# Turning queries and keys of three batches by transposing transfers instead of on TensorE

## The chip, the cores and the metric

The kernel runs on one core of a Trainium2 chip. The metric is the device time of one execution in microseconds (us), from the first to the last instruction as the device counts it. The kernel before was timed three times: 1011.01, 1011.4 and 1011.7 us. One further execution was taken by the hardware profiler; it ran 1008.57 us, and its records span 1006.8 us.

The engines are called as in the profile: PE is TensorE's matmul, PEld its weight load, DVE VectorE, ACT ScalarE, POOL GpSimd, SP SyncE, whose queue issues nearly all DMAs. A letter q after an engine's name is its queue. L252 is line 252 of the kernel before.

## What is computed

Two parts follow each other: attention in which a query sees only the keys that were assigned to the same of 16 centroids, and a feed-forward block with a squared Relu. All tensors are float32.

```python
batch, n_heads, seq, head_dim = (4, 8, 768, 64)
...
q_assign = np.argmax(np.einsum('bhsd,hcd->bhsc', q_n, c_n), axis=-1)
k_assign = np.argmax(np.einsum('bhsd,hcd->bhsc', k_n, c_n), axis=-1)
mask = q_assign[:, :, :, None] == k_assign[:, :, None, :]
scores = scale * np.matmul(q, k.transpose(0, 1, 3, 2))
scores = np.where(mask, scores, -1000000000.0)
...
attn = attn / (np.sum(attn, axis=-1, keepdims=True) + 1e-09)
return np.matmul(attn, v).astype(np.float32)
...
x = np.ascontiguousarray(attn_out.transpose(0, 2, 1, 3)).reshape(B * S, H * D)
h = x @ w_in
r = np.maximum(h, 0.0)
return ((r * r) @ w_out).astype(np.float32)
```

Scores need both queries and keys with the head's 64 columns on the partitions, so each 128x128 piece of q and k has to be turned once. That turning is what the change is about.

## The kernel before

**Pairs and units.** Two heads of one batch make a pair, whose 2 x 64 columns fill the 128 partitions of a turned piece. There are 16 pairs: 0 to 3 belong to batch 0 (HP = 4), 4 to 15 to batches 1 to 3. A pair has 12 pieces of 128 positions, six of q and six of k. The work of a pair is cut into six units (pair, h, c): h is the half of the queries, c = 0, 2, 4 the pair of key pieces. For batch 0 all first halves come before all second halves; from pair 4 on a pair's six units follow each other, which takes some 34 us. Each unit traces its scores (L370), and two units later its product with v (`times_v`, L433).

**A unit.** `scores` makes eight matmuls into two PSUM tiles `sc`, ACT takes the exponential (L397, two instructions of 768 columns), and for batches 1 to 3 DVE masks by comparing cluster numbers (L401, four instructions), from PSUM into `ex`. POOL adds up the masked values (L411, L413). `last_exp` keeps the latest exponential, so that work can be tied behind it on ACT: `tc.issue_after(last_exp[0])` fixes the order of issue on the engine and adds no wait.

**Preparing a pair.** `load_qk` (L100) loads q and k of a pair into two tiles of the pool `loads`, which has four buffers under one tag. `turn` (L245) turns them in three parts: four transposes on PE (L252) into a PSUM tile `pt` and one copy by ACT (L254) into `qkT`; after part 2 it loads the pair after the next. `qkT` has two buffers for these pairs. `logits` (L262) multiplies the turned pieces with the centroids, `route` (L275) finds the number of the nearest one on DVE, and `spread` (L333) writes the numbers as a row to DRAM (L342) and loads them back onto all partitions as `qid` (L343). Batch 0 uses `turn_onehot` instead of `spread`.

**The order of the preparation.** `prep` (L348) returns these steps as a list, and the main loop (L712) takes up to three entries a unit from it, where None takes an entry's place and does nothing. `next_pair` (L688) starts the preparation of pair p + 1 at the first unit of pair p, and that of pair 4 at the second half of pair 3. For pairs after 4 the list is stretched by None entries (L717 to L720): turning in the first unit, logits in the second, route in the third, spread in the fourth.

**Finishing a half.** `add_up` (L460) makes the sums `sm` on PE, their reciprocal `r` on DVE (L482), and carries it through DRAM: SP issues `far_r` (L485), `seen` (L486), waits until far_r has landed, and issues two broadcast loads `rb` (L489). `finish` (L498), a unit later, multiplies by it on DVE (L501) and so fills `xT`, the input of the feed-forward.

**The fill.** The feed-forward of batch 0 (`ffn`, L510) is not run by itself: its matmuls (`ph`, L515, and `po`, L528) are dealt out among the units as filling for PE. `ph` is read by ACT (L522, L523). Its PSUM tiles come from the pool `ps_f`, two banks that `pt`, `lg`, `lt`, `pb`, `sm`, `ph` and `po` share. The feed-forward of batches 1 to 3 (`ffn_pair`, L541, with the matmuls L607 and L638) follows after all attention.

**Who sets the order.** The code gives each engine's instructions in a rough order of priority; a planner orders them by priority and by when it reckons each to be ready, and that order is then fixed. Each engine, SP's queue too, works through its list in order: one that waits holds back all behind it.

Of the kernel before, what the change touches and what calls it, by code (L numbers as in the profile page):

```python
# [8 lines left out]
F32 = mybir.dt.float32  # L9
BF16 = mybir.dt.bfloat16  # L10
I32 = mybir.dt.int32
U32 = mybir.dt.uint32
ALU = mybir.AluOpType
ACT = mybir.ActivationFunctionType
# [3 lines left out]
P = 128  # L18
# [6 lines left out]
def kernel(  # L25
# [10 lines left out]
    nc = tc.nc  # L36

    B, H, S, D = q.shape
    C = centroids.shape[1]
    NCH = S // P  # L40
# [4 lines left out]
    HP = H // 2  # L45
    NB = NCH // 2
    TB = NB * P
    NG = B * HP
# [10 lines left out]
    loads = ctx.enter_context(tc.tile_pool(name="loads", bufs=4))  # L59
    loads_v = ctx.enter_context(tc.tile_pool(name="loads_v", bufs=2))  # L60
    qktp = ctx.enter_context(tc.tile_pool(name="qktp", bufs=2))
# [13 lines left out]
    dram = ctx.enter_context(tc.tile_pool(name="dram", bufs=2, space=bass.MemoryType.DRAM))  # L75
# [21 lines left out]
    raw = {}  # L97
    raw_v = {}

    def load_qk(pair):  # L100
        if pair >= NG:
            return
        b, hp = divmod(pair, HP)
        raw[pair] = []
        for name, src in (("q_raw", q), ("k_raw", k)):
            t = loads.tile([P, NCH, 2 * D], F32, name=name, tag="qk")
            for e in range(2):
                (nc.scalar if pair == 0 and src is k else nc.sync).dma_start(
                    t[:, :, D * e : D * (e + 1)],
                    src[b, 2 * hp + e].rearrange("(p j) d -> p j d", p=P),  # L110
                )
            raw[pair].append(t)
# [15 lines left out]
    for fr in range(DFF // NW):  # L128
        for a in range(KT):
            cols = slice(fr * NW, (fr + 1) * NW)  # L130
# [110 lines left out]
    qkT = {}  # L241
# [3 lines left out]
    def turn(pair, part):  # L245
        if part == 0:
            pool = qkt_early if 2 <= pair < HP else qktp
            qkT[pair] = pool.tile([P, 2 * NCH, P], F32, name="qkT")
        pt = bank("pt", [P, 4, P])
        for i in range(4):  # L250
            which, c = divmod(4 * part + i, NCH)
            nc.tensor.transpose(out=pt[:, i], in_=raw[pair][which][:, c], identity=ident)  # L252
        dst = qkT[pair][:, 4 * part : 4 * part + 4]
        nc.scalar.copy(out=dst, in_=pt)  # L254
        if part == 2:
            raw.pop(pair)
            load_qk(pair + 2)

    lgs = {}
    last_logits = {}  # L260
# [1 line left out]
    def logits(pair):  # L262
        hp = pair % HP
        lg = (bank if pair else first_bank)("lg", [P, TB])
        last_logits[pair] = together(
            dict(
                out=lg[32 * g : 32 * g + 32], lhsT=cnT[:, 2 * C * hp : 2 * C * (hp + 1)],
                rhs=qkT[pair][:, NB * g : NB * (g + 1)], start=True, stop=True,
            )
            for g in range(4)  # L270
        )
        lgs[pair] = once.tile([P, TB], F32, name="lgs")
        nc.scalar.copy(out=lgs[pair], in_=lg)

    def route(pair):  # L275
        with tc.high_priority(offset=2000):
            number(pair)
# [35 lines left out]
    def turn_onehot(pair, which):  # L313
        if pair == 0:
            pt = first_bank("po", [P, NCH, P], BF16)
        else:
            pt = ps_f.tile([P, NCH, P], BF16, name="po", tag="f")
        for c in range(NCH):
            nc.tensor.transpose(
                out=pt[:, c],  # L320
                in_=oh[:, c % NB, 2 * which + c // NB].rearrange("p e c -> p (e c)"),
                identity=ident_b,
            )
        dst = qid[pair][1][:, which]
        src = pt.rearrange("p c n -> p (c n)")
        if which == 0 and pair == 0:
            nc.vector.tensor_copy(out=dst, in_=src)
        elif which == 0:
            nc.scalar.copy(out=dst, in_=src)
        else:  # L330
            nc.scalar.activation(out=dst, in_=src, func=ACT.Copy, bias=-BIG, scale=BIG)

    def spread(pair):  # L333

        src, dst = qid[pair]
        n = 4 * NB
        pb = ps_f.tile([n, P], BF16, name="pb", tag="f")
        nc.tensor.transpose(out=pb, in_=src.rearrange("p g e i -> p (g e i)"), identity=ident_b)
        row = once.tile([n, P], BF16, name="row", tag="b")
        nc.scalar.copy(out=row, in_=pb)  # L340
        far = dram.tile([n, P], BF16, name="far")
        nc.sync.dma_start(far, row)  # L342
        nc.sync.dma_start(  # L343
            dst.rearrange("p g e n -> p (g e n)"),
            far.rearrange("r n -> (r n)").partition_broadcast(P),
        )

    def prep(pair):  # L348
        return [
            lambda: turn(pair, 0), lambda: turn(pair, 1), lambda: turn(pair, 2),  # L350
            lambda: logits(pair), lambda: route(pair),
        ] + (
            [lambda i=i: turn_onehot(pair, i) for i in range(2)] if pair < HP
            else [lambda: spread(pair)]
        )

# [1 line left out]
    last_exp = [None]  # L360
# [327 lines left out]
    def next_pair(u):  # L688

        pair, h, c = units[u]  # L690
        if c == 0 and pair + 1 < NG and h == 0 and (pair + 1) not in qkT:
            if pair + 1 < HP or pair >= HP:
                return pair + 1
        if c == 0 and h == 1 and pair == HP - 1:
            return pair + 1
        return None

    to_round = iter(range(len(weights)))
# [7 lines left out]
    ahead = []  # L706
# [5 lines left out]
    for u in range(len(units) + LAG + 2):  # L712
        if u < len(units):
            pair, h, c = units[u]
            if (p := next_pair(u)) is not None:
                ahead.extend(prep(p))
                if p > HP:  # L717

                    t0, t1, t2, lg, rt, *sp = ahead
                    ahead = [t0, t1, t2, lg, None, None, rt, None, None, *sp]  # L720
            if c == 0 and u + 3 < len(units) and units[u + 3][0] not in raw_v:
                load_v(units[u + 3][0])

            with behind_first(u):
                scores(pair, h, c)
        done = None
        if LAG <= u < len(units) + LAG:
            pair, h, c = units[u - LAG]
            times_v(pair, h, c)
            if c == NCH - 2:  # L730
                done = pair, h

        rounding += 4
        while rounding >= 3:
            rounding -= 3
            i = next(to_round, None)
            if i is not None:
                with tc.issue_after(last_exp[0]):
                    round_weights(i)
                if (i := next(loaded, None)) is not None:  # L740
                    load_weights(i)
            elif not later:
                early.close()
                for name, bufs in (("xT", 5), ("out", 2)):
                    later[name] = keep.enter_context(
                        tc.tile_pool(name=name + "_late", bufs=bufs, side="right",
                                     reuse_waits="tile")
                    )
        share = max(0, left[0] - RESERVE) * density(u) // max(1, sum(map(density, range(u, ENDS))))
        goal = left[0] - share  # L750
        fill_steps(share // 2)
        for _ in range(3):
            if ahead:
                with behind_first(u):
                    (ahead.pop(0) or int)()
        fill_steps(left[0] - goal)

        if not (done and first_half(*done)):
            ended.append(done)
            done = ended.pop(0)  # L760
        if done:
            pair, h = done
            with tc.high_priority(offset=1000) if pair < HP else ExitStack():
                add_up(pair, h)
            if h == 1:
                for d in (qkT, ids, qid):
                    d.pop(pair)
            if h == 1 or pair < HP:
                raw_v.pop(pair)

        now = [done] if done and wide(*done) else []
        added.append(None if now else done)
        for pair, h in now + [d for d in [added.pop(0)] if d]:
            b, hp = divmod(pair, HP)
            with tc.high_priority(offset=1000) if wide(pair, h) else ExitStack():
                finish(pair, h)
            if hp == HP - 1 and (h == 1 or b == 0):
                for half in [(b, h)] if b == 0 else [(b, 0), (b, 1)]:
                    if half in PLAIN:
                        fill.append(ffn(*half))  # L780
# [3 lines left out]
    def check_sums():  # L784
# [20 lines left out]
    wtp, tp, sp, gp = (  # L805
        fast.enter_context(tc.tile_pool(name=name, bufs=1, reuse_waits="tile"))
        for name in ("wtp", "tp", "sp", "gp")
    )
# [207 lines left out]
```

## Time and profile before

| stretch, us from the start | what runs | PE busy | ACT busy | DVE busy | POOL busy | DMA share |
|---|---|---|---|---|---|---|
| 0 to 75 | batch 0, rounding of weights | 67.05 of 75 | 53.45 | 48.15 | 21.61 | 0.83 |
| 75 to 150 | batch 0, rounding of weights | 74.50 of 75 | 46.51 | 59.13 | 53.40 | 0.46 |
| 500 to 560 | last pairs of batches 1 to 3 | 59.68 of 60 | 21.07 | 40.25 | 38.57 | 0.10 |
| 600 to 700 | feed-forward of batches 1 to 3 | 100.00 of 100 | 7.21 | 47.62 | 9.40 | 0.03 |

The stretches between, in which most of the change lies, stand in the prediction. The granted clock of PE is 1.00 throughout. The first matmul of the last stage (L607) starts at 566.53 us.

In lists of instruction groups a row gives line, engine, operation, output and input tile, shapes and count; after the first bar the busy time in us and the mean duration of one in ns; after the second the engine's idle time just before them and what ended it. A row of a timeline gives start and length in us, engine, line and operation, and in brackets the idle time before it with its releaser. A row of waits reads: who waited, for whom, us in total, times, longest.

### The profile page before, as it was taken

Reading aid. Unit: us, or ns where it says so; the run is one execution under the profiler, and the core shown is the slowest. Engines: PE = TensorE matmul, PEld = TensorE weight load, DVE = VectorE, ACT = ScalarE, POOL = GpSimd, SP = SyncE. Lnnn points to the kernel's source line nnn. Section 1 sums busy time; section 2 is a strip of 40 time slices with the busy share of each in tenths; the row PEclk is TensorE's granted clock in tenths of the full one; section 3 lists DMA queues with packets and bytes.
Section 4 is the critical chain, followed back from the end, with each engine's and each line's share of the span. In section 5 each row is a group of like instructions: output and inputs, shape, how many; then the busy total and the mean of one; then the engine's idle time right before and its main releaser. Section 6 shows DMA issues by size and latency. Waiting matters only on the chain.

```text
span 1006.8 us, 12188 instructions
## 1 busy us (share of the span) xinstructions
PE 988.9 (98%) x4583; PEld 555.7 (55%) x4583; DVE 568.6 (56%) x907; ACT 301.0 (30%) x497; POOL 378.0 (38%) x277
## 2 busy tenths in 40 slices
PE   7999999999999999999999999999999999999997
PEld 3444444334443444443333455788655888556886
DVE  4779766655555647564675775623455532566321
ACT  5876565333333453443342111000111000111000
POOL 1338764555555555465566633001232002231000
PEclk9999999999999999999999999999999999999999
DMA  9774442122212220221110000000000000000000
GB/s 246 200 215 151 144 118 72 38 77 64 82 48 66 63 73 25 77 58 48 35 58 17 28 1 1 1 21 21 21 1 0 1 21 32 12 0 1 21 22 24
DMA packets 71512, 55.46 MB, mean 55 GB/s; under 512 B 53274, under 2 KB 62870, under 8 KB 71446
## 3 DMA queue, kind: packets, MB, share of 16 engines
q1 hardware_dynamic: 69734, 54.18, 18.7%
q8 instruction: 38, 0.62, 0.3%
q10 hardware_dynamic: 1712, 0.43, 0.2%
q14 instruction: 28, 0.23, 0.1%
HBM read 48.07 MB, written 6.42 MB: 54 GB/s over the span
## 4 chain that ended last, share of the span: by engine, by line
PE 88%; DVE 5%; DMA 2%; ACT 2%; issue 2%; SPq 0%; POOL 0%; DVEq 0%; ACTq 0%
PE bank L638 22%; PE bank L607 22%; PE po L528 8%; PE ph L515 7%; PE sc L90 7%; PE av L90 6%; PE sc L93 6%; PE av L93 5%; PE pt L252 2%; DVE ex L401 1%; DMA rb<-far_r 1%; PE sm L93 1%; DVE r L482 1%; PE sm L90 1%; ACT ex L397 1%
## 5 line engine op out<-in xcount | busy, mean ns | idle before, releaser
L413 POOL TENSOR_TENSOR acc<-acc,ex 128x768 f32<-128x768 f32 x112 | 208.2, 1859 | 142.0 <-DVE ex L401 127.1
L401 DVE SCALAR_TENSOR_TENSOR ex<-qid,ids,sc 128x384 f32<-128x384 bf16 x288 | 158.2, 607 | 69.6 <-ACT sc L397 67.3
L93 PE MATMUL sc<-qkT 64*128 64x384 f32 x576 | 150.4, 502 | 0.3
L397 ACT ACTIVATE sc<-sc 128x768 f32<-128x768 f32 x144 | 108.0, 792 | 132.9 <-PE sc L93 131.5
L93 PE MATMUL av<-ex,v_raw 128*64 128x384 f32 x576 | 144.4, 495 | 0.0
L577 DVE TENSOR_TENSOR g<-bank,g 128x384 f32<-128x384 f32 x144 | 77.8, 556 | 80.4 <-PE bank L607 79.3
L596 POOL TENSOR_TENSOR w_s<-w_in 128x256 f32<-128x256 f32 x24 | 18.7, 778 | 275.9 <-PE bank L638 162.0
L528 PE MATMUL po<-w_out,gT 128*128 128x512 f32 x192 | 100.9, 627 | 0.0
L515 PE MATMUL ph<-xT,w_in 128*128 128x384 f32 x256 | 96.9, 506 | 2.2 <-DVE r L482 2.2
L638 PE MATMUL bank<-w_out,g 128*128 128x256 f32 x432 | 95.2, 379 | 0.0
L638 PEld LDWEIGHTS bank<-w_out,g 128*128 128x128 f32 x432 | 82.1, 190 | 11.8
L90 PE MATMUL sc<-qkT 64*128 64x384 f32 x192 | 87.2, 534 | 0.2 <-DVE ex L401 0.2
L577 DVE TENSOR_TENSOR osb<-bank,osb 128x256 f32<-128x256 f32 x54 | 22.1, 423 | 107.6 <-PE bank L638 102.2
L90 PE MATMUL av<-ex,v_raw 128*64 128x384 f32 x192 | 82.5, 512 | 0.0
L93 PEld LDWEIGHTS sc<-qkT 64*128 64x128 f32 x576 | 65.0, 186 | 26.3 <-issue 1.1
L515 PEld LDWEIGHTS ph<-xT,w_in 128*128 128x128 f32 x256 | 44.0, 189 | 47.1 <-issue 16.3
L607 PE MATMUL bank<-xT,w_in 128*128 128x384 f32 x192 | 69.9, 487 | 0.0
L607 PE MATMUL bank<-x_t,w_s 128*128 128x384 f32 x192 | 69.8, 486 | 0.0
L607 PE MATMUL bank<-xT,w_s 128*128 128x384 f32 x192 | 69.8, 486 | 0.0
L411 POOL TENSOR_TENSOR acc<-ex 128x768 f32<-128x768 f32 x28 | 50.8, 1814 | 47.4 <-DVE ex L401 36.1
L638 PE MATMUL bank<-w_t,g_s 128*128 128x256 f32 x288 | 65.1, 379 | 0.0
L638 PE MATMUL bank<-w_t,g 128*128 128x256 f32 x288 | 65.1, 379 | 0.0
(121 smaller groups left out, 1214.8 us busy)
## 6 DMA issues: line engine op xcount, KB each, us to landing
w_raw<-in_moe_w_in_dram SPq DMA_DIRECT2D x16, 512.0 KB
w_raw<-in_moe_w_out_dram SPq DMA_DIRECT2D x16, 512.0 KB
v_raw<-in_v_dram SPq DMA_DIRECT2D x20, 384.0 KB
q_raw<-in_q_dram SPq DMA_DIRECT2D x32, 192.0 KB
rb<-far_r SPq DMA_DIRECT2D x62, 96.0 KB
out_dram<-osb SPq DMA_DIRECT2D x23, 256.0 KB
k_raw<-in_k_dram SPq DMA_DIRECT2D x30, 192.0 KB
qid<-far SPq DMA_DIRECT2D x12, 384.0 KB
```

Source lines behind the costliest of these rows:

```text
L90: last = nc.tensor.matmul(**next(products))
L93: last = nc.tensor.matmul(**product)
L252: nc.tensor.transpose(out=pt[:, i], in_=raw[pair][which][:, c], identity=ident)
L397: last_exp[0] = nc.scalar.activation(out=t[:, 2 * i : 2 * i + 2] if pair < HP else src, in_=src, func=ACT.Exp, scale=SCALE).ins
L401: nc.vector.scalar_tensor_tensor(out=t[:, 2 * i + e], in0=qid[pair][1][:, h, e], scalar=ids[pair][:, ch % NB, 2 + ch // NB, e : e + 1], in ...
L411: nc.gpsimd.tensor_tensor(out=acc[pair, h], in0=t[:, 0:2], in1=t[:, 2:4], op=ALU.add)
L413: nc.gpsimd.tensor_tensor(out=acc[pair, h], in0=acc[pair, h], in1=t[:, 2 * i : 2 * i + 2], op=ALU.add)
L515: nc.tensor.matmul(ph, lhsT=w_in[:, kk, f * P : (f + 1) * P], rhs=xT[b, h][:, kk], start=(kk == 0), stop=(kk == KT - 1),)
L528: nc.tensor.matmul(po, lhsT=gT[f][:, i * P : (i + 1) * P], rhs=w_out[:, f], start=(f == 0), stop=(f == FT - 1),)
L577: nc.vector.tensor_tensor(out=out, in0=bank, in1=to, op=ALU.add)
L607: nc.tensor.matmul(bank, lhsT=operands[j][0][:, kk], rhs=operands[j][1][:, kk], start=(kk == 0), stop=(kk == H2 - 1),)
L638: nc.tensor.matmul(bank, lhsT=operands[j][0][:, f], rhs=operands[j][1][:, f], start=(f == 0), stop=(f == F2 - 1),)
```

## The change

For pairs 4 to 15 the transposes on PE and their copies on ACT go. In their place each 32-bit word of q and k is split into its two 16-bit halves, the halves are written to DRAM, and one transposing DMA for a pair brings them back turned:

- `split_words(pair, which)`, once for q and once for k: two copies on ACT take the low and the high halves of each row apart into a tile `flat` (each 128 x 3 x 2 x 128 halves, so 768 a partition), from every other 16-bit element of the loaded tile. Both are tied behind the latest exponential. SP then writes `flat` to the DRAM tensor `words`, 393 KB. `flat` takes buffers of the same four as the loads. After k the loads of the next pair follow.
- `turn_words(pair)`: one transposing DMA issued by SP reads the 3072 rows of 128 halves of a pair (786 KB) and writes them to `qkT`, where the two halves of a word come to lie side by side again.
- `prep` for these pairs becomes a list by itself: in the first unit `turn_words` and the splitting of the next pair's q, in the third logits and the splitting of the next pair's k, in the fourth route, in the fifth spread. Before, logits stood in the second unit, route in the third, spread in the fourth.
- Pair 4's words are split at units 12 and 15, and its preparation starts three units earlier, at the second half of pair 2. `turn` loads the pair after the next only for pairs 0, 1 and 2; from then on each `split_words` of k loads the next pair.

```diff
-            load_qk(pair + 2)
+            if pair in (0, 1, HP - 2):
+                load_qk(pair + 2)
...
+    def split_words(pair, which):
+        if which == 0:
+            words[pair] = dram.tile([2 * NCH, P, 2, 2 * D], U16, name="words")
+        flat = loads.tile([P, NCH, 2, 2 * D], U16, name="flat", tag="qk")
+        src = raw[pair][which].bitcast(U16).rearrange("p c (d two) -> p c two d", two=2)
+        half = NCH // 2
+        with tc.issue_after(last_exp[0]):
+            for cols in (slice(0, half), slice(half, NCH)):
+                nc.scalar.copy(out=flat[:, cols], in_=src[:, cols])
+        nc.sync.dma_start(
+            words[pair][NCH * which : NCH * (which + 1)].rearrange("c p two d -> p c two d"),
+            flat,
+        )
+        if which == 1:
+            raw.pop(pair)
+            load_qk(pair + 1)
+
+    def turn_words(pair):
+        qkT[pair] = qktp.tile([P, 2 * NCH, P], F32, name="qkT")
+        nc.sync.dma_start(
+            qkT[pair].rearrange("p c n -> p (c n)").bitcast(U16),
+            words.pop(pair).rearrange("c p two d -> (c p two) d"), transpose=True,
+        )
...
     def prep(pair):
...
+        split = [lambda i=i: split_words(pair + 1, i) for i in range(2 if pair + 1 < NG else 0)]
+        first, second = split or (None, None)
         return [
-            lambda: turn(pair, 0), lambda: turn(pair, 1), lambda: turn(pair, 2),
-            lambda: logits(pair), lambda: route(pair),
-        ] + (
-            [lambda i=i: turn_onehot(pair, i) for i in range(2)] if pair < HP
-            else [lambda: spread(pair)]
-        )
+            lambda: turn_words(pair), None, first, None, None, None,
+            lambda: logits(pair), None, second, lambda: route(pair), None, None,
+            lambda: spread(pair),
+        ]
...
-        if c == 0 and h == 1 and pair == HP - 1:
-            return pair + 1
+        if c == 0 and h == 1 and pair == HP - 2:
+            return HP
...
-                if p > HP:
-
-                    t0, t1, t2, lg, rt, *sp = ahead
-                    ahead = [t0, t1, t2, lg, None, None, rt, None, None, *sp]
+            if u in (HP * NCH // 2, HP * NCH // 2 + 3):
+
+                split_words(HP, int(u > HP * NCH // 2))
```

More of the change, by code (lines that the diff above doesn't have):

```diff
@@ L11 @@
 I32 = mybir.dt.int32
+U16 = mybir.dt.uint16
 U32 = mybir.dt.uint32
@@ L256, in turn @@
             raw.pop(pair)
-            load_qk(pair + 2)
+            if pair in (0, 1, HP - 2):
+                load_qk(pair + 2)
+    words = {}
+    def split_words(pair, which):
[20 more added lines that the diff above has]
+        )
     lgs = {}
@@ L348, in prep @@
     def prep(pair):
-        return [
-            lambda: turn(pair, 0), lambda: turn(pair, 1), lambda: turn(pair, 2),
-            lambda: logits(pair), lambda: route(pair),
-        ] + (
-            [lambda i=i: turn_onehot(pair, i) for i in range(2)] if pair < HP
-            else [lambda: spread(pair)]
-        )
+        if pair < HP:
+            return [
+                lambda: turn(pair, 0), lambda: turn(pair, 1), lambda: turn(pair, 2),
+                lambda: logits(pair), lambda: route(pair),
+                lambda: turn_onehot(pair, 0), lambda: turn_onehot(pair, 1),
+            ]
+        split = [lambda i=i: split_words(pair + 1, i) for i in range(2 if pair + 1 < NG else 0)]
+        first, second = split or (None, None)
+        return [
+            lambda: turn_words(pair), None, first, None, None, None,
+            lambda: logits(pair), None, second, lambda: route(pair), None, None,
+            lambda: spread(pair),
+        ]
     ex = {}
```

## The prediction

> **What bounds the kernel now.** I read the engine totals first, then the table of stretches, to see whether TensorE is full in the stretch where the change works.
>
> ```profile
> PE 988.9 (98%) x4583; PEld 555.7 (55%) x4583; DVE 568.6 (56%) x907; ACT 301.0 (30%) x497; POOL 378.0 (38%) x277
> 150.00:250.00 100.00, 98.94 (x481) 40.05 (x481) 62.02 (x101) 39.66 (x63) 54.34 (x31) 1.00 0.23 63
> 250.00:300.00 50.00, 50.00 (x244) 20.10 (x242) 27.93 (x48) 17.79 (x27) 27.76 (x16) 1.00 0.21 59
> 300.00:400.00 100.00, 98.27 (x490) 42.41 (x486) 58.94 (x95) 44.08 (x73) 52.22 (x29) 1.00 0.23 61
> 400.00:500.00 100.00, 99.13 (x488) 40.55 (x488) 59.46 (x99) 38.06 (x60) 53.77 (x31) 1.00 0.19 55
> ```
>
> In the rows of stretches the columns after start, end and length are busy us of PE, PEld, DVE, ACT, POOL, then clock, DMA share, GB/s. From 150 to 500 us PE idles 3.7 us of 350 (1.06 + 0 + 1.73 + 0.87). DVE is at about 60%, POOL at 54%, ACT at 40%, DMA at 20%. The attention of batches 1 to 3 is bound by PE, whose gaps the feed-forward of batch 0 fills: work taken off PE there should come off the end, as long as nothing new makes PE wait.
>
> Next, what the turned tiles cost PE: the groups, then one pair in the timeline (start, length).
>
> ```profile
> L252 PE MATMUL pt<-ident,k_raw 128*128 128x128 f32 x96 | 16.6, 289 | 0.3 <-ACT qkT L254 0.3
> L252 PE MATMUL pt<-ident,q_raw 128*128 128x128 f32 x96 | 16.4, 289 | 6.1 <-DMA q_raw<-in_q_dram 6.1
> L254 ACT COPY qkT<-pt 128x512 f32<-128x512 f32 x48 | 27.8, 592 | 35.9 <-PE pt L252 35.9
> ...
> 367.22 0.60 PE L252 MATMUL pt<-ident,q_raw 128*128 128x128 f32 x4
> 369.24 0.44 PE L252 MATMUL pt<-ident,q_raw 128*128 128x128 f32 x2
> 369.52 0.82 PE L252 MATMUL pt<-ident,k_raw 128*128 128x128 f32 x6
> 370.27 0.54 PE L90 MATMUL av<-ex,v_raw 128*64 128x384 f32 x1
> ```
>
> The mean of 289 ns is latency; they are pipelined. From the start at 369.24 to the next other matmul at 370.27, 8 transposes take 1.03 us, 129 ns each. The same start-to-start reading over the timeline from 130 us on gives 15.8 us for 131 of them, 120 ns each.
>
> Last, the place most open to harm: SP's order, and what waits for it.
>
> ```profile
> 364.42 0.53 SPq L485 DMA_DIRECT2D far_r<-r  x1
> 365.00 0.55 SPq L486 DMA_DIRECT2D seen<-r  x1
> 366.04 1.12 SPq L489 DMA_DIRECT2D rb<-far_r  x2
> ...
> 369.37 0.56 DVE L501 SCALAR_TENSOR_TENSOR xT<-av,rb 128x384 f32<-128x384 f32 x1 [2.44 <-DMA rb<-far_r]
> 369.84 2.18 DVE L401 SCALAR_TENSOR_TENSOR ex<-qid,ids,sc 128x384 f32<-128x384 bf16 x4
> ...
> DVE xT L501 <- DMA rb<-far_r: 54.4, 22, 5.0
> ```
>
> The reciprocals travel SBUF, DRAM, SBUF. DVE stands idle for rb at L501, 22 times and 54.4 us between 150 and 560 us, with the masking of the next scores (L401) queued behind it. Today that hardly reaches PE.
>
> **What the Trainium skill says.** "DMA: Bandwidth & Descriptors", section "DMA Transpose (X-bar)": the plain transposing DMA takes 2-byte elements only and goes through SP's or ACT's queue. So 32-bit words must be split into halves, and the transfer stands in one of the two queues; no run of before shows one. Same page, "Latency and other measured facts": 261 GB/s for such a transfer with a non-contiguous middle dimension, 350 to 400 when contiguous. The trace has only plain loads: the 256-byte rows of q and k move at some 260 to 290 GB/s in the busy slices from 437 to 446 us. Same page, "Issuing engines are not separate DMA queues": all transfers share the 16 engines; the trace agrees in that q1 carries 54.18 of 55.46 MB, far_r, rb and qid among them. "VectorE: DVE Perf Modes", "The three transpose paths": 1309 ns by DMA for one 128x128 bf16 tile, 390 ns on TensorE; this trace has 273 ns (median, f32) on TensorE.
>
> **Part by part.**
>
> *Removed from PE:* 12 pairs (4 to 15) x 12 transposes = 144 x 120 ns = **17.3 us**, all where PE is full. Their three ACT copies a pair go too (36 x 592 ns = 21.3 us of ACT), and their three turns in the two shared PSUM banks.
>
> *Added on ACT:* four copies of 128x768 halves a pair. No row shows one. From PSUM, 768 elements take 792 ns and 384 take 491, so 0.78 ns an element. A copy in SBUF reading every other word takes 690 ns for 512 (L151); 256 more make 0.89 us. Bounds: 0.82 us (523 ns of L523 for 384 plus 384 x 0.78) and 1.02 us (1.3 ns an element, from L523 to L151). I take 0.89: 3.6 us a pair against 1.8 removed, +21 us of ACT in all, at 40% busy. What counts is place: two copies, 1.8 us, right behind the exponentials of two units of six. The next exponentials come 3.5 us later or more (368.84 + 1.50 to 376.52 is 6 us), so scores don't wait. Queued behind the copies is the Relu (L522) that frees a bank for ph. Where ph is being filled, both banks turn over each 4 matmuls; after 308 us and before 175 that is some five pairs, so ten blocks. Bounds: 0 (the Relu lands in a gap) and 10 x 1.8 = 18 us. I take 3, since the pt tiles no longer compete for these banks. Where po is filled, a bank lasts 16 matmuls and nothing waits.
>
> *Added on SP and DMA:* a pair writes 786 KB of halves to DRAM in two issues and reads them back in one transposing transfer. Two issues at 0.3 to 0.65 us hide in SP's gaps: its issues fill some 8 us of a pair's 34. The writes move at about 280 GB/s, 1.4 us each. The transfer: 786 KB at 261 GB/s is an estimate of **3.0 us**; bounds 2.0 (390 GB/s) and 31.4 us (24 tiles x 1309 ns, one after another). DMA time a pair rises by 2.8 + 3.0 of 34 us, 17%, onto 20%: no bound.
>
> *What waits for it:* logits of the pair, two units after turn_words, so 11 us and more at some 5.5 us a unit. 3 us plus two or three of latency hide there. The transfer cannot start before the last scores on the old qkT buffer, which end at 364.4 in the pair shown: the moment far_r goes out. So turn_words is ready just while SP waits for far_r to land, and it can slip in ahead of rb. How much may rb be late? With the 1.03 us of transposes gone the next scores come at 375.46 - 1.03 = 374.4; their first tile needs two maskings (1.1 us), so L401 must start by 373.3 and rb land by 372.8, against 369.37 today: **3.4 us of slack**. 3.0 us fits, narrowly; I book 1 us in all. For the other half of a pair (h = 1), rb lands at 353.53 and a 1.4 us write of words stands against about 2 us of slack.
>
> *Moved:* load_qk of the next pair goes one pair ahead instead of two, but still some four units before its copies: nothing. Spread comes one unit later (fourth instead of third of six) with two units left to land 384 KB, which go in about 2 us at 421 to 427: nothing. Preparing pair 4 three units earlier falls into the weight rounding; SP waits at L138 are up to 7.1 us there and happen once: 0 to 5 us, I take 0, as two units last 14 us.
>
> *Sum:* -17.3 + 3 + 1 = **-13.3 us**: the span of 1006.8 becomes 993.5. That profiled run took 1008.6 us, the timed ones 1011.0 to 1011.7; on their median of 1011.4 I forecast **998**.
>
> **Rivals.**
>
> *A: the transfer holds back rb (slower).* Place: turn_words between far_r and rb, on SP or in the rings. Price: the transfer's length beyond 3.4 us, 12 times. It eats the whole gain from 3.4 + 17.3/12 = 4.8 us on, 162 GB/s. At half the skill's rate, 6 us: 12 x 2.6 = 31 us against 17.3, so 1011.4 + 14 = **1025**. For it: far<-row already slips between seen and rb at 387.42, and no run of before shows what turning costs beyond a plain load of the same rows. Against: half of the halves' rb (those of h = 1) are issued two units later, and at 391.51 xT stands behind three maskings without a wait.
>
> *B: copies in ACT's way (small gain).* The Relus behind copies cost PE ten times 1.2 us: 1011.4 - 17.3 + 12 = **1006**. For it: ACT serves both banks and the scores in one queue. Against: 60% idle.
>
> *C: transposes one tile at a time.* 31.4 us a pair against some 13 us until logits: 12 x 18 = 220 us, about **1215**. For it: the 1309 ns. Against: that is one small tile, whose latency needn't add up.
>
> *D: nothing comes off.* PE's gaps return elsewhere: **1011**. For it: the waits for rb on DVE. Against: 3.7 us of idle in 350, with fill at hand.
>
> **How the numbers follow.** Forecast 0.50 (992 to 1003), B 0.14 (1003 to 1009), D 0.06, A 0.25 (1014 to 1050), C 0.05. A measurement of this kernel tells about 0.2%, 2 us, from no change. Faster 0.50 + 0.14 = 0.64; same 0.06; slower 0.25 + 0.05 = 0.30. Range 991 to 1030: above it lie C and about half of A, below it 2 in 100. The likeliest case alone: 992 to 1003.
>
> **What would show it.** Right: no L252 after 150 us, PE still 98% or more busy to 500 us, the first matmul of L607 near 553 instead of 566.5 us, ACT copies of 0.8 to 1.0 us, waits for rb on DVE not much above 54 us. A: transposing transfers over 5 us, rb issued behind them, PE waiting for L401. B: PE waits for L522. C: PE waits at lg. The forecast is wrong if PE's idle time between 150 and 560 us grows by more than 10 us.

## The result and the profile after

The changed kernel takes 994.58 us (median of 4 runs, 994.2 to 997.46), the kernel before 1011.54 us beside it. The ratio is 0.9839, with a 95% interval from 0.9821 to 0.9858: 17.0 us faster. The forecast was 998, with 992 to 1003 for its own case.

The two profiled executions differ by less: spans of 1006.8 and 992.6 us, 14.2 us; a second profile of the changed kernel, taken later, spans 991.0 us, 15.8 us less than before. In some executions PE's first matmuls take about twice as long and all that follows comes 3.0 us later (shown in the last section): these three profiles don't have that, while most timed executions of before probably do and most of after don't, which only their times suggest. So 14.2 to 15.8 us is the like-for-like gain; where a span below has those 3.0 us in it, the text says so.

The totals and the stretches of the changed kernel; the columns after start, end and length are busy us of PE, PEld, DVE, ACT, POOL, then clock, DMA share, GB/s. Line numbers are now those of the changed kernel, 38 further down in the part after `turn_words` (L553 is L515 of before, L439 is L401, L527 is L489, L539 is L501).

```profile
PE 973.4 (98%) x4439; PEld 540.7 (54%) x4439; DVE 561.7 (57%) x907; ACT 315.9 (32%) x509; POOL 377.4 (38%) x277
150.00:250.00 100.00, 97.47 (x457) 37.50 (x457) 65.44 (x103) 44.80 (x66) 56.16 (x32) 1.00 0.44 108
250.00:300.00 50.00, 49.22 (x223) 17.93 (x222) 29.35 (x50) 19.54 (x28) 27.69 (x16) 1.00 0.49 116
300.00:400.00 100.00, 99.98 (x485) 42.37 (x486) 57.30 (x99) 50.88 (x81) 55.29 (x31) 1.00 0.46 113
400.00:500.00 100.00, 99.08 (x469) 37.16 (x470) 65.07 (x107) 41.49 (x61) 57.50 (x32) 1.00 0.39 98
```

PE has 144 instructions fewer and 15.5 us less to do (988.9 to 973.4), and idles 4.3 us of the 350, against 3.7 before. So nearly all that left PE came off the end: the first matmul of the last stage (L645, before L607) starts at 551.99 instead of 566.53 us, 14.5 us earlier. ACT has 15 us more, and the DMA share doubled to 0.39 to 0.49; neither is anywhere near full.

The instructions of the change, from the lists of what touches the tiles `flat` and `qkT`; after the count come the shortest, median and longest duration in ns:

```profile
L274 ACT COPY flat<-q_raw x24: 814/836/848, 73.4 to 456.2; 128x768 uint16<-128x768 uint16 x24
L275 SPq DMA_DIRECT2D words<-flat x24: 378/400/582, 79.4 to 466.8; - x24
L285 SPq DMA_TRANSPOSE qkT<-words x12: 3099/3805/4917, 102.8 to 482.5; - x12
```

A copy takes 0.84 us. The transposing transfer occupies SP's queue for 3.8 us at the median, where plain loads take 0.3 to 0.75 at their medians (a few up to 3 us): nothing else is issued from it in that time.

Where it stands, in the timeline of the changed kernel around the switch from one pair to the next (start and length in us):

```profile
350.64 0.59 PE L94 MATMUL sc<-qkT 64*128 64x384 f32 x1
352.24 4.02 SPq L285 DMA_TRANSPOSE qkT<-words  x1
355.70 0.35 PE L91 MATMUL sm<-acc,ups 128*32 128x192 f32 x1
356.16 0.59 PE L91 MATMUL sc<-qkT 64*128 64x384 f32 x1
357.68 0.54 SPq L523 DMA_DIRECT2D far_r<-r  x1
358.27 0.53 SPq L524 DMA_DIRECT2D seen<-r  x1
358.52 1.56 ACT L274 COPY flat<-q_raw 128x768 uint16<-128x768 uint16 x2
359.31 1.12 SPq L527 DMA_DIRECT2D rb<-far_r  x2
...
362.69 0.56 DVE L539 SCALAR_TENSOR_TENSOR xT<-av,rb 128x384 f32<-128x384 f32 x1 [2.49 <-DMA rb<-far_r]
```

The last scores of the old pair (350.64) free the buffer, the transfer goes out at once and lets SP go at 356.26, and only at 357.68 does SP send far_r. The two do not meet. In all ten pairs from 6 on the transfer starts 4.8 to 6.3 us ahead of far_r; only pair 5's, at 144.89, stands between seen and rb. DVE's waits for rb between 150 and 560 us are 42.8 us in 15, fewer than before.

### The profile page after: what moved, and what is told of

It reads as the page before. It is cut to its first block, busy times and chain, and to the rows that moved or that the text cites. A ratio compares the mean times of both kernels' runs of the same rounds, so it can differ in the third digit from the quotient of the medians.

```text
span 992.6 us, 12019 instructions
## 1 busy us (share of the span) xinstructions
PE 973.4 (98%) x4439; PEld 540.7 (54%) x4439; DVE 561.7 (57%) x907; ACT 315.9 (32%) x509; POOL 377.4 (38%) x277
## 3 DMA queue, kind: packets, MB, share of 16 engines
q1 hardware_dynamic: 125798, 73.06, 28.1%
## 4 chain that ended last, share of the span: by engine, by line
PE 92%; DVE 2%; DMA 2%; ACT 2%; issue 1%; SPq 0%; DVEq 0%; ACTq 0%
PE bank L676 22%; PE bank L645 22%; PE po L566 9%; PE ph L553 8%; PE sc L91 7%; PE av L91 7%; PE sc L94 7%; PE av L94 6%; PE sm L94 1%; PE sm L91 1%; PE lg L91 1%; PE lt L314 1%; ACT ex L435 1%; DMA rb<-far_r 1%; DVE ex L439 1%
## 5 line engine op out<-in xcount | busy, mean ns | idle before, releaser
L451 POOL TENSOR_TENSOR acc<-acc,ex 128x768 f32<-128x768 f32 x112 | 205.7, 1837 | 113.1 <-DVE ex L439 100.4
L439 DVE SCALAR_TENSOR_TENSOR ex<-qid,ids,sc 128x384 f32<-128x384 bf16 x288 | 158.5, 606 | 68.3 <-ACT sc L435 59.2
L553 PE MATMUL ph<-xT,w_in 128*128 128x384 f32 x256 | 96.3, 506 | 0.5 <-DVE r L520 0.5
L645 PE MATMUL bank<-xT,w_in 128*128 128x384 f32 x192 | 69.9, 487 | 0.0
L645 PE MATMUL bank<-x_t,w_s 128*128 128x384 f32 x192 | 69.8, 486 | 0.0
L645 PE MATMUL bank<-xT,w_s 128*128 128x384 f32 x192 | 69.8, 486 | 0.0
L553 PEld LDWEIGHTS ph<-xT,w_in 128*128 128x128 f32 x256 | 44.3, 189 | 46.7 <-issue 20.1
L520 DVE RECIPROCAL r<-sm 128x192 f32<-128x192 f32 x31 | 42.0, 1355 | 48.6 <-PE sm L94 48.6
```

Of the source, the lines that this page charges most:

```text
L439: nc.vector.scalar_tensor_tensor(out=t[:, 2 * i + e], in0=qid[pair][1][:, h, e], scalar=ids[pair][:, ch % NB, 2 + ch // NB, e : e + 1], in ...
L451: nc.gpsimd.tensor_tensor(out=acc[pair, h], in0=acc[pair, h], in1=t[:, 2 * i : 2 * i + 2], op=ALU.add)
L520: nc.vector.reciprocal(out=r, in_=sm)
L553: nc.tensor.matmul(ph, lhsT=w_in[:, kk, f * P : (f + 1) * P], rhs=xT[b, h][:, kk], start=(kk == 0), stop=(kk == KT - 1),)
L645: nc.tensor.matmul(bank, lhsT=operands[j][0][:, kk], rhs=operands[j][1][:, kk], start=(kk == 0), stop=(kk == H2 - 1),)
```

## The experiments

Theory 1: the gain is PE's time for the transposes; all that was added lies beside it. Against it stood the schedule (theory 3), the freed banks (theory 4), and the two costs that the prediction named: rb held back behind the transfer (A) and copies in ACT's way (B).

**The transposes alone.** In the kernel before, for pairs 4 to 15:

```diff
-        pt = bank("pt", [P, 4, P])
-        for i in range(4):
-            which, c = divmod(4 * part + i, NCH)
-            nc.tensor.transpose(out=pt[:, i], in_=raw[pair][which][:, c], identity=ident)
...
-        nc.scalar.copy(out=dst, in_=pt)
+        if pair >= HP:
+            q_r, k_r = raw[pair]
+            if part == 0:
+                nc.scalar.copy(out=dst, in_=q_r[:, 0:4])
+            elif part == 1:
+                nc.scalar.copy(out=dst[:, 0:2], in_=q_r[:, 4:6])
+                nc.scalar.copy(out=dst[:, 2:4], in_=k_r[:, 0:2])
+            else:
+                nc.scalar.copy(out=dst, in_=k_r[:, 2:6])
...
```

> The kernel before with one thing taken out: PE's 144 transposes of pairs 4 to 15. The copies on ACT read the loaded tile in place of pt (four a pair instead of three, since one straddles q and k), so the queries and keys of these pairs stay unturned. No halves, no words, no transposing transfer. Theory 1 (the gain is PE's time for the transposes, 17.3 us, and everything that the change adds lies beside it at 0 to 4 us): 1011.5 - 17.3 = 994, between 991 and 996, and the changed kernel of 994.6 is no more than 2 us away. Theory 2 (the added copies, writes and transfers cost something that a larger gain covers): 991 or less. Theory 3 (the gain comes from the changed schedule and not from PE's time): 1003 or more.

Measured: 996.86 us median, ratio 0.9853 (0.983 to 0.9875), with a span of 991.2 us. The median lies 0.9 us above my 991 to 996 and 2.3 us above the changed kernel; two of the five executions gave 993, three 997 to 998. By the spans that is 15.6 us under the span of before, and 1.4 us under the changed kernel's first profile, 0.2 us over its second. PE is busy 18.1 us less than before and idles 5.8 us of the 350 instead of 3.7:

```profile
PE 970.8 (98%) x4439; PEld 540.9 (55%) x4439; DVE 571.8 (58%) x907; ACT 301.3 (30%) x509; POOL 377.8 (38%) x277
```

> The changed kernel as it is, beside the two others on one chip: 992 to 997.

That run gave 995.58 us, ratio 0.9851 (0.9817 to 0.9884). So 24 writes, 12 transfers and the moved steps, with 48 copies of halves in place of the 48 plain copies that this kernel has on ACT, cost 0 to 1.4 us together; what copies cost by themselves is tested below. Theory 2 is out.

**PE's time put back.** Four transposes go into each of three tiles `pt` that nobody reads:

```diff
+        def idle_turn():
+            pt = bank("pt", [P, 4, P])
+            for i in range(4):
+                nc.tensor.transpose(out=pt[:, i], in_=ident, identity=ident)
...
-            lambda: turn_words(pair), None, first, None, None, None,
+            lambda: turn_words(pair), idle_turn, first, idle_turn, idle_turn, None,
```

> The changed kernel with PE's work put back and nothing else: in the first two units of each preparation 12 transposes of the identity into three pt banks that nobody reads. ACT gets no copies for them. Theory 1 (PE's time is the gain): 994.6 + 17.3 = 1012, between 1009 and 1014. Theory 4 (the gain is that pt, its copies and the shared banks are out of the way, and PE's time alone would be hidden): 1000 or less.

The first line of the page and the group of the added transposes:

```profile
PE 989.9 (98%) x4583; PEld 555.2 (55%) x4583; DVE 564.0 (56%) x907; ACT 315.7 (31%) x509; POOL 377.1 (37%) x277
L390 PE MATMUL pt<-ident 128*128 128x128 f32 x144 | 21.8, 274 | 1.0 <-DVE r L525 1.0
```

Measured: 1009.4 us, ratio to before 0.9974 (0.9962 to 0.9986); span 1007.4, 14.8 and 16.4 us over the changed kernel's two profiles. PE's work rises by 16.5 us and the end by nearly as much: 103 to 114 ns a transpose. The tiles `pt` take the shared banks again, if only for the length of the transposes, but PE doesn't wait more for that: it idles 2.8 us from 150 to 500 us, against 4.3 in the changed kernel. Theory 1 holds and theory 4 falls. It is PE's time, from both sides: 15.6 us taken out of before, 14.8 to 16.4 put into after.

**The schedule alone.** The changed kernel's order of preparation with the turning back on PE:

```diff
-            if pair in (0, 1, HP - 2):
-                load_qk(pair + 2)
+            load_qk(pair + 2)
...
-            lambda: turn_words(pair), None, first, None, None, None,
-            lambda: logits(pair), None, second, lambda: route(pair), None, None,
+            lambda: turn(pair, 0), lambda: turn(pair, 1), lambda: turn(pair, 2), None, None, None,
+            lambda: logits(pair), None, None, lambda: route(pair), None, None,
...
-                split_words(HP, int(u > HP * NCH // 2))
```

> The changed kernel's order of preparation (pair 4 three units earlier, logits, route and spread one unit later each) with the turning put back on PE and its copies on ACT, loads two pairs ahead as before. It computes the same as the kernel before. Theory 1 (only PE's time counts): the same as before, 1011.5 within 2 us. Theory 3 (the schedule gives part of the gain): 1003 to 1008.

Measured: 1011.11 us, ratio 0.9993 (0.9978 to 1.0008). The span is 1008.5 us, 1.7 over that of before. The moved steps by themselves gain nothing.

**Rival B: the copies twice.**

```diff
-                nc.scalar.copy(out=flat[:, cols], in_=src[:, cols])
+                for _ in range(2):
+                    nc.scalar.copy(out=flat[:, cols], in_=src[:, cols])
```

> The changed kernel with each of the four copies of halves a pair made twice, one behind the other: 3.3 us of ACT more a pair, 3.1 us more behind the exponentials in two units of six. Theory 1 (the copies lie in ACT's free time): the same, 994.6 to 997. Rival B of the prediction (the copies hold back the Relus that free the banks of ph, some ten times): the second copy costs at least as much as the first, 10 x 1.2 us or more: 1003 to 1010.

The stretch in which ph is filled, so where both banks turn over fastest:

```profile
300.00:400.00 100.00, 99.97 (x482) 41.95 (x481) 58.58 (x102) 57.85 (x91) 54.37 (x30) 1.00 0.44 110
```

Measured: 996.25 us, ratio 0.984 (0.9818 to 0.9862), the changed kernel's. ACT is busy 57.85 us of 100 instead of 50.88, PE 99.97 as before. Its span of 994.5 us, less the 3.0 us of its start, is 991.5. Behind the exponentials, 3.3 us of copies cost as little as 1.7. B is out.

**The tie taken away.**

```diff
-        with tc.issue_after(last_exp[0]):
+        with ExitStack():
```

> The changed kernel without the tie of the copies of halves behind the exponentials; they then stand in ACT's order where the planner reckons them ready. Theory 1 (the copies lie in ACT's free time, at 40 to 50% busy): the same, 993 to 998. Rival: a copy ahead of the exponentials holds the scores back 1.6 us in up to 24 units: 1000 to 1030.

Measured: 1021.93 us, ratio 1.0089 (1.0063 to 1.0116), so 27 us over the changed kernel; the rival's side. In the stretches, the waits, and the timeline of ACT:

```profile
75.00:150.00 75.00, 64.81 (x289) 29.28 (x286) 46.72 (x40) 46.70 (x77) 41.97 (x26) 0.93 0.89 228
150.00:250.00 100.00, 89.84 (x401) 35.44 (x400) 59.77 (x87) 54.07 (x86) 50.22 (x30) 0.95 0.55 142
400.00:500.00 100.00, 99.99 (x486) 39.15 (x484) 58.71 (x101) 36.98 (x59) 57.62 (x32) 1.00 0.24 63
...
ACT flat L274 <- DMA q_raw<-in_q_dram: 21.7, 6, 8.3
...
111.78 0.83 ACT L274 COPY flat<-q_raw 128x768 uint16<-128x768 uint16 x1 [8.26 <-DMA q_raw<-in_q_dram]
```

The loss is not the 1.6 us of copying that the rival named. The planner puts the copies several pairs ahead, and ACT then stands 21.7 us waiting for q loads that are late behind the weights' loads, with exponentials and Relus queued behind. PE idles 10.2 us of 75 and 10.2 of 100 there, where the changed kernel's PE idles 0.6 and 2.5, and its granted clock sinks to 0.93 and 0.95. Its matmuls, as many as in the changed kernel, are busy 983.6 us instead of 973.4, so about 10 of the 28.1 us between the spans are slower matmuls and the rest is waiting. From 400 to 500 us PE is full. In the changed kernel no copy waits for a load.

To see whether the tie matters only early, it was kept for pairs 4 to 7 alone:

```diff
-        with tc.issue_after(last_exp[0]):
+        with tc.issue_after(last_exp[0]) if pair < HP + 4 else ExitStack():
```

> The changed kernel with the tie behind the exponentials kept for pairs 4 to 7 alone; from pair 8 on the copies stand where the planner reckons them ready, as in the untied kernel. Theory (the untied copies cost in batch 0 and at its end, where a copy waits in ACT's queue for a load that is late behind the weights' loads; later they cost nothing): as the changed kernel, 0 to 3 us less, 992 to 996. If the tie is needed throughout, the untied kernel's loss comes back in part: 1000 or more.

Measured: 1000.72 us, ratio 0.9892 (0.9865 to 0.9919), 5.1 us over the changed kernel beside it, and 7.6 by the two spans (998.6 and 991.0). My expectation failed. The waits of its copies:

```profile
ACT flat L274 <- DMA q_raw<-in_q_dram: 10.0, 3, 7.3
ACT flat L274 <- DMA k_raw<-in_k_dram: 8.5, 4, 3.0
```

The same wait appears where the tie ends: from pair 8 on the planner at once draws several pairs' copies forward, to where their loads are not there yet, although the last weights were loaded by 140 us; so late weights are not needed for it. PE idles 6.4 us from 150 to 250 and 2.7 from 250 to 300, and 0.2 in the 200 us after. So what the tie buys here is that a copy never stands in ACT's queue ahead of its load.

**Rival A: the transfer between seen and rb.** For pairs 6 to 15 the order far_r, seen, transfer, rb is written in (`sent` is the DMA to seen):

```diff
+            if h == 0 and HP <= pair < NG - 2:
+                with tc.issue_after(sent):
+                    turned = turn_words(pair + 2)
+                behind = tc.issue_after(turned)
+            with behind:
...
                 nc.sync.dma_start(rb[D * e : D * (e + 1)], far[e].partition_broadcast(D))
```

> The changed kernel with rival A's order written in: for pairs 6 to 15 SP issues far_r, seen, then the transposing transfer, then rb. The same work. In the changed kernel the transfer went out 5.5 us ahead of far_r, as soon as the last scores on the old buffer were done, and so was over. Theory 1 with rival A's mechanism: SP is held 3.8 us (median record of the transfer), so rb goes out some 3.3 us later; in the changed kernel xT has about 2 us until PE's next scores need the masking behind it, so 1 to 2 us of waiting ten times: 1005 to 1015, with PE waiting for L439 or the xT line. If the transfer is hidden anyway: 994 to 997.

SP's timeline at one switch of pairs, what DVE then does, and PE's waits:

```profile
265.77 0.53 SPq L523 DMA_DIRECT2D far_r<-r  x1
266.35 0.55 SPq L524 DMA_DIRECT2D seen<-r  x1
267.00 2.97 SPq L285 DMA_TRANSPOSE qkT<-words  x1
270.07 1.18 SPq L533 DMA_DIRECT2D rb<-far_r  x2
...
274.06 0.56 DVE L545 SCALAR_TENSOR_TENSOR xT<-av,rb 128x384 f32<-128x384 f32 x1 [2.44 <-DMA rb<-far_r]
...
PE sc L91 <- DVE ex L439: 11.5, 12, 2.0
```

Measured: 1011.5 us, ratio to before 0.9974 (0.9961 to 0.9988). The same work in another order on SP takes the whole gain back. rb goes out 4.3 us after far_r instead of 1.6, and PE waits for the masking 11.5 us in 12 waits instead of 2.9 in 4; no wait of PE for `qkT` appears. Its span of 1009.9 us, less the 3.0 us of its start, is 14.3 us over the changed kernel's first profile, 1.4 us for each of ten pairs. Rival A's mechanism is real, its price as expected; the changed kernel just doesn't have it.

**The transfer twice.**

```diff
-        nc.sync.dma_start(
+        for _ in range(2):
+            nc.sync.dma_start(
...
```

> The changed kernel with each transposing transfer made twice into the same tile. The second waits on SP until the first has landed, so SP is held some 9 us a pair where 5.5 us are free ahead of far_r. Theory 1: the time of the transfer counts only beyond that gap; rb late by some 3 us in most pairs against 2 us of slack: 997 to 1008. If the transfer's own time were on the path already: 3.8 us more for each of 12, 1040. If it is hidden wherever it stands: 994 to 997.

SP, and DVE at one switch of pairs:

```profile
306.14 10.74 SPq L286 DMA_TRANSPOSE qkT<-words  x2
316.93 0.54 SPq L525 DMA_DIRECT2D far_r<-r  x1
318.98 1.14 SPq L529 DMA_DIRECT2D rb<-far_r  x2
...
323.65 0.56 DVE L541 SCALAR_TENSOR_TENSOR xT<-av,rb 128x384 f32<-128x384 f32 x1 [7.10 <-DMA rb<-far_r]
```

Measured: 1037.95 us, ratio 1.0245 (1.0225 to 1.0264): 43 us over the changed kernel, far above my 997 to 1008, or 3.6 us for each of 12 pairs. That comes near the 1040 of the case in which the transfer's own time is on the path, but the trace shows another cause: the two hold SP for 10.7 us, r is ready at 310.15, far_r goes out 6.8 us late, and PE's scores wait for the masking behind it, up to 6.1 us. I had put 9 us against 5.5 free ones. Nor is all of it waiting. The first line is this kernel's, the second that of the copies twice, which has as many matmuls and the same start; PEclk is the granted clock of this kernel in 40 slices of the span, where 9 is 0.9 or more and 8 is 0.8 or more:

```profile
PE 992.8 (96%) x4439; PEld 545.1 (52%) x4439; DVE 562.3 (54%) x907; ACT 316.9 (30%) x509; POOL 377.2 (36%) x277
PE 975.8 (98%) x4439; PEld 541.7 (54%) x4439; DVE 562.2 (57%) x907; ACT 348.9 (35%) x557; POOL 378.0 (38%) x277
PEclk9999999999998998999999999999999999999999
```

From 150 to 560 us the granted clock is 0.96 on average, against 1.00 there. Of the 44.5 us between the two spans (1039.0 and 994.5) 17.0 are slower matmuls and 27.5 idle time, so, as an estimate, a pair pays 2.3 us of waiting for the 6 us by which the two transfers outlast the free 4 to 5, and 1.4 us of lower clock.

**The transfer without turning.** Four plain loads of the pair's q and k into the same tile:

```diff
-            qkT[pair].rearrange("p c n -> p (c n)").bitcast(U16),
-            words.pop(pair).rearrange("c p two d -> (c p two) d"), transpose=True,
...
+                    qkT[pair][:, NCH * i : NCH * (i + 1), D * e : D * (e + 1)],
+                    src[b, 2 * hp + e].rearrange("(p j) d -> p j d", p=P),
```

> The changed kernel with the transposing transfer of a pair replaced by four plain loads of the pair's q and k into the same tile, 768 KB in rows of 256 bytes. Copies and writes of the halves stay, but nobody reads them, and the pieces stay unturned. Theory 1 (the transfer lies beside PE's work): the same as the changed kernel within 2 us, with SP held some 2.5 us (four issues of 0.6) instead of 3.8. If the turning itself cost time on the path: 4 us less or more.

Measured: 992.1 us, ratio 0.9804 (0.9779 to 0.9828). The median is 3.5 us under the changed kernel's beside it, more than the 2 us that I allowed, but the latter's six executions spread from 992.8 to 1001.9. The profiles span 990.6 us here and 991.0 and 992.6 in the changed kernel. Turning as such costs 0.4 to 2.0 us by the spans. The four loads hold SP some 2.5 us a pair (medians of 0.59 and 0.64 each).

**One pair more.** Pair 3 of batch 0 split at units 4 and 5 and turned at unit 6:

```diff
+            if u in (4, 5):
+                split_words(HP - 1, u - 4)
```

> The changed kernel with pair 3 of batch 0 turned by a transposing transfer as well: 12 transposes fewer, split at units 4 and 5, turned at unit 6, logits and the rest two units before its first scores. Theory 1 (PE's time is what counts): 12 x 0.12 = 1.4 us less, 993. Against it: in the first 75 us the DMA engines are at 0.77 of their time and PE is not full, so landing late costs 2 to 8 us: 997 to 1003.

Measured: 1010.7 us, ratio 0.9977 (0.9959 to 0.9995). The 1.4 us saved on PE cost some 16, more than either expectation. PE waits 5.2 us for `qkT` at the logits in one wait, the feed-forward then waits 4.6 us for a reciprocal; between the units that start at 54 and 81 us in the changed kernel it falls 15 us behind, and the granted clock is 0.98 and 0.93 in the first two stretches of 75 us. How the rest of the 15 us divides was not taken apart. Here, where PE is not full and the loads are late, the transfer had nothing to hide behind. No version here that computes the same beats the changed kernel.

## Why the prediction was right

**The bound was read rightly.** PE was full from 150 to 500 us, fill took up every gap, and PE's time came off the end almost one for one: 15.5 us less work, 14.2 to 15.8 us less span. D and theory 3 had nothing to stand on.

**The first term was some 1.7 us too large.** I took 144 x 120 ns = 17.3 us from the distance of starts. That distance holds, at each group's end, the change to another kind of matmul, which PE pays with or without transposes: in the trace of before a transpose starts 109 ns after the one ahead of it (median, 150 to 500 us) and scores 203 ns after the last transpose, but scores also start 416 ns after a matmul of ph, where the next of ph starts after 323. The 93 ns more are the same in both, and 144 x 109 ns are 15.7 us. The runs say 15.6 us (taken out) and 14.8 to 16.4 (put back), 103 to 114 ns each.

**Copies: size right, price too high.** 0.84 us measured against 0.89 estimated. The 3 us booked for them were zero, as far as these runs can tell: twice the copies costs nothing either. What I had not seen is that their place is worth far more than their length. I asked only what is queued behind a copy, not what the copy itself waits for; untied, that wait costs 27 us, the lower clock that came with it included.

**The transfer: 3.8 us, not 3.0, and it holds SP.** "DMA: Bandwidth & Descriptors", section "Latency and other measured facts", gave 261 GB/s. One transfer of the changed kernel has the DMA engines nearly to itself, the last one, issued at 482.53 us. What they moved from 480 to 488 us, in slices of 0.2 us (the first hump, up to slice 16, is the load of qid):

```profile
GB/s 0 0 0 0 0 0 77 169 307 246 353 246 200 169 154 46 0 0 3 101 61 122 109 164 260 289 289 292 294 288 288 288 291 292 294 178 112 0 0 0
```

The transfer's part runs from 483.6 to 487.4 us: about 1.2 us at 61 to 164 GB/s, then some 290 GB/s, as fast as plain loads of 256-byte rows. 786 KB in 3.8 us are 207 GB/s, under the page's figure because of that slow beginning; the part after it is above the 261 and under the 350 to 400. Rival C's 24 x 1309 ns, from "VectorE: DVE Perf Modes", section "The three transpose paths", doesn't add up that way: 24 tiles took 3.8 us. And SP itself is occupied 3.1 to 4.9 us. My sum priced two of the three issues on SP and for the third only its transfer; it named SP as a place for rival A but gave the hold no length.

**The place was off by one unit.** I wrote that the last scores on the old buffer end at 364.4, as far_r goes out. Those scores, which start at 362.89 in the trace of before, are the first of the next pair: the sums of the old pair's half stand directly ahead of them. The old pair's last scores are those at 357.37, a unit earlier, and so the transfer gets 5 us of SP to itself. The 1 us I booked came out right by that mistake, which is luck; had the two met, as I assumed, the price would have been 14 us, since the slack is not the 3.4 us that I worked out: rb 2.7 us later already costs 1.4 us a pair. Rival A's mechanism and sign were right, its place wrong, and its chance of 0.25 was too high for a reason that the trace of before held.

**What it said one would see.** No transposes after 150 us, PE busy 98.8% of the time from there to 500 us, the last stage near 553 us (551.99), copies of 0.8 to 1.0 us (0.84), waits for rb not above 54 us (42.8): all five. The sum of -13.3 us lies near the like-for-like 14.2 to 15.8 in part because its errors offset each other: 1.7 us too much gain against 4 us booked for costs that come to 0 to 1.4. That the median fell to 994.6 and not to 998 is for the rest probably the start of the executions.

## What to carry to other kernels

If one engine is full and has fill for its gaps, work taken off it comes off the end, and what replaces it is judged by its place in each queue and not by its length: the same transfer was free ahead of the small loads and cost 14 us between them, and the same copies were free behind the exponentials and cost 27 us where they stood waiting for their own loads. For each instruction that joins an in-order queue ask two things: who stands behind it, and what it waits for itself. To find the moment of a buffer's release, name the last reader in the trace by its neighbours, since an error of one unit there can turn the verdict: it is the difference between no cost and 14 us here.

## What was not expected of the hardware

**The start has two speeds.** Six matmuls of the first unit's scores, in the changed kernel and in the one with rb behind the transfer, where nothing differs in that part:

```profile
12.39 1.55 PE L94 MATMUL sc<-qkT 64*128 64x384 f32 x6
```

```profile
13.84 2.93 PE L94 MATMUL sc<-qkT 64*128 64x384 f32 x6
```

The same six matmuls take 1.55 or 2.93 us, though the clock is recorded as 1.00 in both; from some 20 us on they are equal again and all is 3.0 us later. Of the 13 profiled executions four show the longer start: the copies twice, the transfer twice, rb behind the transfer, and pair 3. What decides it was not looked into. A difference of 3 us between two times of this kernel therefore needs a look at the start.

**Waiting can cost the clock too.** In the untied kernel the granted clock fell to 0.93 and 0.95 in the two stretches where PE idled 10.2 us each, with the transfer twice it was 0.96 from 150 to 560 us, and about 10 of 28 and 17 of 44 us of these losses are slower matmuls. Idle time alone doesn't do it: with rb behind the transfer PE idled 5.9 us from 150 to 250 us and the clock stayed at 1.00. There no wait after the first matmul was longer than 2.0 us, while these two kernels have single waits of up to 3.7 and 6.1 us. Whether it is the length of a wait that decides was not tested.

**A transposing transfer occupies the issuing queue** for 3.8 us at the median for 786 KB. Four plain loads of as many bytes took some 2.5 us together, in four pieces of about 0.6, so what differs most is that the transfer holds the queue in one piece.
